# Decode attention on one core: PV moved ahead of the scores, wo split and loaded late, the FFN later

One core of a Trainium2 chip. The metric is the device time of one execution in microseconds. On a single core a run is called slow when it lies over 1.5% above the fastest of the same kernel in the same call; ratios use fast runs only. PE is TensorE, DVE VectorE, ACT ScalarE. The granted clock is the share of PE's full clock that the profile gives for a stretch. A transfer is said to have landed when the last of its 16 completions stands in the trace.

## The reference, cut

Two tokens (batch 2, one position each), 32 heads, a cache of 4096 keys and values per head, head width 128, bfloat16:

```python
q = (x @ wq)                                   # 2 x 512 -> 2 x 32 heads x 128
scores = einsum("bhqd,bhkd->bhqk", q, k_cache) * 128 ** -0.5
p = softmax(scores);  o = einsum("bhqk,bhkd->bhqd", p, v_cache)
a = o.reshape(2, 1, 4096) @ wo                 # 4096 -> 512
b = relu(x @ w1) @ w2                          # 512 -> 1376 -> 512
return g * a + (1 - g) * b                     # g = sigmoid(sum(x * gate_w))
```

K and V are 64 slabs each of 1 MiB (one per batch and head). With wq and wo (4 MiB each), w1 and w2, some 145 MB have to come from HBM.

## The kernel before

A key slab lands as 32 blocks of 128 x 128. PE transposes each block into PSUM (four banks, eight blocks a bank), DVE and ACT copy the banks to `kt`, PE multiplies each transposed block with q (one column), and the softmax of four heads is done together. PV uses the V slab as it landed. Work is laid out in units, one head per unit: in unit k PE does the scores of head k-1, PV of head k-7, and the transposes of head k.

```python
for k in range(NUNITS):                        # PE
    if 1 <= k <= NH:
        unit_scores(k - 1, 0)                  # waits for the copies of head k-1
        unit_scores(k - 1, 1)
    for step, off in (("a", 1), ("b", 2), ("c", 3), ("d", 4)):
        ...                                    # one small softmax matmul in a unit
    unit_pv(k - G - DLY)                       # head k-7: 32 one-column matmuls
    if k < NH:
        unit_trans(k, 0); unit_trans(k, 1)     # 32 transposes
    if k == U_FFN: ffn_setup()                 # U_FFN = 3
pe.wait_ge(S["oT_done"], 1)
for h in range(Hq):                            # all of wo after the last PV
    last = pe.matmul(ATB[0:Bn, 0:D], lhsT=oT_sb[:, h : ... : Hq], rhs=wo_sb[:, h, :], ...)
```

The queue of SyncE issues the loads. A K slab waits for a free buffer out of six, which PE frees; the V slab of head k-6 follows the K slab of head k:

```python
for k in range(NH):
    if k >= NE and (k - NE) - NKR >= 0:
        sp.wait_ge(S["kfree"], k - NKR + 1)    # PE has begun the transposes of head k-5
    sp.dma_start(kdst, kslab(k)).then_inc(ks, 16)
    if k == min(U_FFN - 2, NH - 1): ...        # w1, w2 behind K1
    kv = k - OFFV
    if kv >= 0: issue_v(kv)
```

wo is loaded by ACT's queue as the first thing of the program.

## Time and profile before

| | before |
|---|---|
| time, median of the 4 runs at first | 399.88 us (394.69 to 405.19) |
| time, median of the 16 runs in the end | 405.44 us (394.69 to 411.09) |
| span of the profiled run (the fastest one) | 393.0 us |
| PE busy / granted clock | 85% / 0.716 |
| HBM read | 145.4 MB, 370 GB/s over the span |

From 40 to 340 us PE is busy 90 to 93% of the time and the DMA all of it, so the busy shares decide nothing.

Each run lists its granted clock, and over those of the kernel before the time goes with the clock: 394.69 us at 0.716, 399.12 at 0.708, 403.18 at 0.680.

### The profile page before, as it was taken

To read this page: it belongs to the slowest core of one execution; us is meant where nothing else is said; L and a number is where in the kernel's file an instruction comes from. 1 tells how busy PE (TensorE), PEld (TensorE's weight loads), DVE (VectorE), ACT (ScalarE), POOL (GpSimd) and SP (SyncE) were. 2 spreads that over 40 slices of the span, in tenths; PEclk is the share of its full clock that TensorE was granted. 3 is DMA by queue.
4 is the path that set the end of the run, shared out by engine and by line. 5 is a ranking of instruction groups with operands and counts; after the bars stand their busy time and mean duration, and the time that the engine had idled before them with its cause. 6 is when DMAs were issued, how large, how long until landed. Compare 5 with 4: busy or idle time off the path is not lost.

```text
span 393.0 us, 13993 instructions
## 1 busy us (share of the span) xinstructions
PE 334.4 (85%) x6459; PEld 316.2 (80%) x6459; DVE 163.5 (42%) x326; ACT 73.9 (19%) x184; POOL 1.1 (0%) x8
## 2 busy tenths in 40 slices
PE   0191699899999899999899999999999999998996
PEld 0191678899898899899898989898989898898862
DVE  0030337254434545354545444454545354543511
ACT  1031123221213111221213131312121221213110
POOL 1000000000000000000000000000000000000000
PEclk9997599566857756656868686868685656865658
DMA  8999999999999999999999999999999999999000
GB/s 299 409 386 363 422 420 417 417 419 418 418 419 422 415 419 412 387 389 381 389 404 411 415 409 409 417 403 407 410 415 408 402 386 372 369 419 396 18 3 0
DMA packets 25079, 146.33 MB, mean 372 GB/s; under 512 B 2135, under 2 KB 7613, under 8 KB 8125
## 3 DMA queue, kind: packets, MB, share of 16 engines
q1 hardware_dynamic: 20908, 141.24, 88.9%
q10 hardware_dynamic: 4112, 4.19, 3.3%
q8 instruction: 51, 0.84, 0.8%
q14 instruction: 8, 0.06, 0.0%
HBM read 145.43 MB, written 0.00 MB: 370 GB/s over the span
## 4 chain that ended last, share of the span: by engine, by line
PE 71%; ACT 12%; SPq 7%; DVE 4%; DMA 3%; issue 2%; ACTq 0%; DVEq 0%
PE trb L301 44%; PE otb L372 15%; ACT kt L441 12%; PE scb L329 6%; SPq L221 5%; DMA vnat<-in_A_k_cache_dram 3%; DVE kt L495 3%; PE smb L405 2%; PE smb L356 2%; SPq L220 1%; PE smb L345 1%; PE smb L276 1%; PE smb L352 1%; PE smb L348 0%; PE otb L264 0%
## 5 line engine op out<-in xcount | busy, mean ns | idle before, releaser
L495 DVE COPY kt<-trb 128x1024 bf16<-128x1024 bf16 x207 | 139.6, 690 | 157.2 <-PE trb L301 156.2
L301 PE MATMUL trb<-ident,knat 128*128 128x128 bf16 x1920 | 176.7, 276 | 0.1
L301 PEld LDWEIGHTS trb<-ident,knat 128*128 128x128 bf16 x1920 | 164.3, 128 | 0.4 <-issue 0.3
L441 ACT ACTIVATE kt<-trb 128x1024 bf16<-128x1024 bf16 x49 | 50.2, 1024 | 267.3 <-PE trb L301 267.3
L329 PE MATMUL scb<-qb,kt 128*128 128x1 bf16 x2048 | 75.9, 166 | 26.0 <-ACT kt L441 19.1
L329 PEld LDWEIGHTS scb<-qb,kt 128*128 128x128 bf16 x2048 | 69.0, 102 | 32.9 <-ACT kt L441 24.4
L372 PE MATMUL otb<-pg,vnat 128*128 128x1 bf16 x768 | 23.6, 165 | 0.0
L372 PE MATMUL otb<-pg,vx_wq 128*128 128x1 bf16 x768 | 23.4, 164 | 0.0
L301 PE MATMUL trb<-ident,vnat 128*128 128x128 bf16 x128 | 14.3, 313 | 10.1 <-DMA vnat<-in_A_k_cache_dram 10.1
L372 PEld LDWEIGHTS otb<-pg,vnat 128*128 128x128 bf16 x768 | 21.6, 100 | 0.9
L372 PEld LDWEIGHTS otb<-pg,vx_wq 128*128 128x128 bf16 x768 | 21.4, 99 | 0.7
L301 PEld LDWEIGHTS trb<-ident,vnat 128*128 128x128 bf16 x128 | 13.3, 148 | 10.2 <-issue 10.2
L452 ACT ACTIVATE pg<-scb,negmax 128x32 bf16<-128x32 f32 x64 | 18.3, 331 | 14.0 <-DVE negmax L521 13.9
L249 PE MATMUL otb<-xT_sb,vx_wq 128*128 128x2 bf16 x128 | 3.5, 165 | 15.9 <-DMA vx_wq<-in_A_wq_dram 15.9
L249 PEld LDWEIGHTS otb<-xT_sb,vx_wq 128*128 128x128 bf16 x128 | 3.5, 104 | 15.9 <-issue 15.9
L372 PE MATMUL otb<-pg,vx_w 128*128 128x1 bf16 x512 | 15.7, 165 | 0.0
L372 PEld LDWEIGHTS otb<-pg,vx_w 128*128 128x128 bf16 x512 | 14.4, 100 | 0.6
L535 DVE COPY recipB<-smb 128x4 f32<-128x4 f32 x16 | 2.6, 162 | 29.0 <-PE smb L356 29.0
L452 ACT ACTIVATION_READ_ACCUMULATOR pg<-scb,negmax 128x1 f32 x64 | 12.9, 202 | 0.0
L405 PE MATMUL smb<-wo_sb,oT_sb 128*2 128x512 bf16 x32 | 9.3, 460 | 0.3 <-DVE oT_sb L563 0.3
L521 DVE TENSOR_SCALAR negmax<-smb 128x4 f32<-128x4 f32 x16 | 2.6, 162 | 13.3 <-PE smb L348 13.3
L405 PEld LDWEIGHTS smb<-wo_sb,oT_sb 128*2 128x2 bf16 x32 | 3.1, 98 | 6.1 <-issue 3.2
(41 smaller groups left out, 61.8 us busy)
## 6 DMA issues: line engine op xcount, KB each, us to landing
knat<-in_A_k_cache_dram SPq DMA_DIRECT2D x60, 1024.0 KB, 8.1
vnat<-in_A_v_cache_dram SPq DMA_DIRECT2D x24, 1024.0 KB, 10.2
vx_wq<-in_A_v_cache_dram SPq DMA_DIRECT2D x24, 1024.0 KB, 11.5
vx_w<-in_A_v_cache_dram SPq DMA_DIRECT2D x16, 1024.0 KB, 10.9
wo_sb<-in_A_wo_dram ACTq DMA_DIRECT2D x1, 4096.0 KB, 41.7
vx_wq<-in_A_wq_dram SPq DMA_DIRECT2D x1, 4096.0 KB, 16.7
vnat<-in_A_k_cache_dram SPq DMA_DIRECT2D x4, 1024.0 KB, 17.2
vx_w<-in_B_w_dram SPq DMA_DIRECT2D x1, 1376.0 KB, 27.6
```

What stands on the lines that cost most here:

```text
L220: sp.dma_start(w2_sb[:, 0 : FC - 1, :], w2_main).then_inc(S["ld_w2"], 16)
L221: sp.dma_start(w2_sb[0:FW_LAST, FC - 1, :], w2_tail).then_inc(S["ld_w2"], 16)
L249: last = pe.matmul(PSQ[:, h * Bn : (h + 1) * Bn], lhsT=wq_sb[:, c, h * Dh : (h + 1) * Dh], rhs=xT_sb[:, c * Bn : (c + 1) * Bn], start=(c = ...
L276: last = pe.matmul(PSF[0:Bn, 0:D], lhsT=h1T_sb[0:fw, fc * Bn : (fc + 1) * Bn], rhs=w2_sb[0:fw, fc, :], start=(fc == 0), stop=(fc == FC - 1),)
L301: ins = pe.transpose(TRB[r][:, (jj % 8) * P : (jj % 8 + 1) * P], kb_ap[:, jj * Dh : (jj + 1) * Dh], ident[:, :],)
L329: ins = pe.matmul(bank[:, hg * NBLK + jj : hg * NBLK + jj + 1], lhsT=kt[kk % NKT][:, jj, :], rhs=qb[:, kk : kk + 1], start=True, stop=True,)
L356: pe.matmul(SMB[:, COL_RB : COL_RB + G], lhsT=ones_f[0:G, :], rhs=rdiag[g % 2][:, :], start=True, stop=True).then_inc(S["rbc"], 1)
L372: last = pe.matmul(OTB[:, kp : kp + 1], lhsT=vnat[kp % NVR][:, jj * Dh : (jj + 1) * Dh], rhs=pg[gp % 2][:, jj, hg : hg + 1], start=(jj == ...
L405: last = pe.matmul(ATB[0:Bn, 0:D], lhsT=cols, rhs=wo_sb[:, h, :], start=(h == 0), stop=(h == Hq - 1),)
L441: act.activation(out=kt[k % NKT][:, i * 8 : (i + 1) * 8, :].rearrange("p a b -> p (a b)"), in_=TRB[r][:, :], func=ACT.Copy,).then_inc(trdo ...
L452: act.activation(out=pg[g % 2][:, :, hg], in_=SCB[g % 2][:, hg * NBLK : (hg + 1) * NBLK], func=ACT.Exp, bias=negmax[:, g * G + hg : g * G ...
L495: dve.tensor_copy(out=kt[k % NKT][:, i * 8 : (i + 1) * 8, :].rearrange("p a b -> p (a b)"), in_=TRB[r][:, :],).then_inc(trdone[r], 1)
```

## The change

Its intent: take away PE's waits for the copies, take work out of the tail, and get the K slabs ahead of the weights at the start. From the ninth unit on, PV and the softmax step come before the scores. The wo product is cut in two: heads 0 to 27 of both batches after PV(59), four heads at the end; its accumulator moves to a PSUM bank of the transposes, which are done by then. The wo load is issued by ACT in its unit 46. The FFN runs after unit 6, with w1 behind K4 and w2 behind K5. The rest is bookkeeping (chunks of eight blocks in place of halves, the FFN's output in another bank, an added semaphore). Cut to the core:

```diff
-    U_FFN = 3
+    U_FFN = 6
...
-                if k == min(U_FFN - 2, NH - 1):
+                if k == min(4, NH - 1):
                     sp.dma_start(w1_sb[:], w1_v).then_inc(S["ld_w1"], 16)
+                if k == min(5, NH - 1):
                     sp.dma_start(w2_sb[:, 0 : FC - 1, :], w2_main).then_inc(S["ld_w2"], 16)
...
             for k in range(NUNITS):
-                if 1 <= k <= NH:
-                    unit_scores(k - 1, 0)
-                    unit_scores(k - 1, 1)
-                for step, off in (...): ... softmax_pe(step, kk // G)
-                unit_pv(k - G - DLY)
+                first = k <= G + DLY
+                if first:
+                    ... scores_chunk(k - 1, qi); softmax_pe(step, kk // G)
+                for qi in range(NQ):
+                    pv_chunk(k - G - DLY, qi)
+                if not first:
+                    ... softmax_pe(step, kk // G); scores_chunk(k - 1, qi)
+                if HA > 0 and k - G - DLY == NH - G - 1:
+                    pe.wait_ge(S["oTA"], 1)
+                    pe.wait_ge(S["ld_wo"], 16)
+                    pe.wait_ge(trdone[0], NFILL_SLOT0)
+                    wo_stage(0, HA)
...
-            act.dma_start(wo_sb[:], wo_v).then_inc(S["ld_wo"], 16)      # first instruction of ACT
+                if k == min(46, NH - 1):
+                    act.dma_start(wo_sb[:], wo_v).then_inc(S["ld_wo"], 16)
...
+                if HA > 0 and k == NH + DLY - 1:                         # DVE
+                    dve.wait_ge(S["pvh"], NH - G)
+                    dve.wait_ge(S["rcp"], NG - 1)
+                    dve.tensor_tensor(out=oT_sb[:, 0 : NH - G], in0=OTB[:, 0 : NH - G],
+                                      in1=recipB[:, 0 : NH - G], op=ALU.mult).then_inc(S["oTA"], 1)
```

## The prediction

> **What bounds the kernel now.** I read the page's 40 slices first, then the waits, the windows, the timeline of two heads, and the tail.

> The slices show two engines that are both nearly full:

> ```profile
> PE   0191699899999899999899999999999999998996
> PEclk9997599566857756656868686868685656865658
> DMA  8999999999999999999999999999999999999000
> GB/s 299 409 386 363 422 420 417 417 419 418 418 419 422 415 419 412 387 389 381 389 404 411 415 409 409 417 403 407 410 415 408 402 386 372 369 419 396 18 3 0
> ```

> One slice is 9.8 us. The transfers run up to slice 37 and stop at about 364 us, so the last 29 us (to 393.0) move nothing: a pure tail. In between GB/s is about 419 for a while, then 370 to 410. The busy share of the DMA stays at 1.0 through both, so it cannot tell which side limits. The windows can:

> ```profile
> core 0: us, PE busy (x) PEld busy (x) DVE busy (x) ACT busy (x) POOL busy (x), PEclk, DMA share, GB/s
> 40.00:150.00 110.00, 99.36 (x1888) 94.40 (x1889) 49.65 (x98) 23.84 (x59) 0.00 (x0) 0.70 1.01 419
> 150.00:190.00 40.00, 37.16 (x695) 36.21 (x693) 18.23 (x36) 6.31 (x13) 0.00 (x0) 0.62 1.00 392
> 190.00:300.00 110.00, 101.74 (x2093) 98.23 (x2090) 54.54 (x110) 23.51 (x64) 0.00 (x0) 0.75 1.01 408
> 300.00:340.00 40.00, 36.95 (x721) 35.90 (x720) 17.62 (x36) 8.12 (x20) 0.00 (x0) 0.66 1.00 388
> ```

> GB/s follows the granted clock of TensorE (0.62 and 0.66 give 392 and 388; 0.75 gives 408). One head needs one K and one V slab, 2.10 MB. At 419 GB/s that is 5.0 us; at 388 it is 5.4 us. So from 150 us on PE sets the pace (it frees the K buffers), and from 40 to 150 us the DMA, with a backlog, runs at what I take for its full rate, 419 GB/s. The waits agree: the queue that issues K slabs waits for PE, not the other way round.

> ```profile
> SPq L217 <- PE trb L301: 236.7, 54, 5.6
> ```

> What PE does in a head at half clock (timeline, one unit):

> ```profile
> 356.03 3.57 PE L301 MATMUL trb<-ident,knat 128*128 128x128 bf16 x32
> 359.39 0.82 PE L329 MATMUL scb<-qb,kt 128*128 128x1 bf16 x24
> 360.72 0.38 PE L329 MATMUL scb<-qb,kt 128*128 128x1 bf16 x8 [0.50 <-ACT kt L441]
> 361.14 1.01 PE L372 MATMUL otb<-pg,vnat 128*128 128x1 bf16 x32
> 362.01 3.17 PE L301 MATMUL trb<-ident,knat 128*128 128x128 bf16 x32
> ```

> The unit lasts 362.01 - 356.03 = 5.98 us. The scores follow their own transposes at once, so the last eight wait for the last copy of the transposed keys (ACT, 1.02 us). Over the run:

> ```profile
> PE scb L329 <- ACT kt L441: 19.1, 38, 0.5
> PE scb L329 <- DVE kt L495: 5.7, 27, 0.2
> ```

> Together 24.8 us, 0.39 us a head.

> [...] every stretch of one clock is a multiple of 3.41 us. [...] Windows cut at these boundaries, transposes alone:

> ```profile
> 193.94:197.36 3.42, 1.74 (x18) 1.47 (x15) 0.50 0.97 333
> 197.36:200.77 3.41, 2.96 (x28) 2.96 (x29) 0.50 1.00 408
> 200.77:204.18 3.41, 0.88 (x15) 0.73 (x14) 1.00 1.02 425
> 204.18:207.60 3.42, 2.67 (x27) 2.41 (x24) 0.50 1.02 407
> 207.60:211.01 3.41, 1.79 (x32) 1.79 (x32) 1.00 1.00 413
> ```

> 28 transposes in a window: the next is full speed. 15: the next is half. 27: full. Over all windows the border is near 22 transposes in 3.41 us[...]. [...]

> **The change, part by part.** From the eighth unit on the order is PV(k-7), softmax steps, scores(k-1), transposes(k). All matmuls stay; only where they stand moves.

> (a) Wait of the scores. The copies of head k-1 now have PV (0.86 us to the next stream) and the softmax step in front of the scores. The third DVE copy ends in time, and the ACT copy (1.02 us after about 0.2) ends before the scores come to its eight blocks (0.86 + 24 x 0.027 = 1.5 us). Removed: nearly all of the 24.8 us. The unit at half clock becomes 3.41 (32 x 107 ns) + 0.86 + 0.86 + 0.24 (mean of the softmax steps) = 5.37 us; at full clock 1.82 + 0.86 + 0.86 + 0.2 = 3.7 us.

> (b) Clock. Before, the non-transpose part of a unit at full clock was 2.7 us or more, so a window could hold as few as 13 transposes and the clock fell. Now it is 1.9 us, so any window at full clock and without starving holds at least (3.41 - 1.9)/1.82 x 32 = 26. At half clock the gap of 1.96 us moves through the windows, and at least one window in three holds over 22. So PE runs at 3.7 us per head whenever K is there, less than the 5.0 us of the DMA: the bound passes to the DMA, and PE then waits for K landings.

> (c) DMA floor. Bytes are unchanged, 146.33 MB: 349.2 us at 419 GB/s. Add what cannot be had back: the first 10 us at 298 GB/s lose 2.9 us, and the loads with short rows (slices 3 and 4 at 383 and 368 GB/s, w1, w2, wo) lose 2.1 us. Last V slab landed: 355 us, against 364. So of 25 us of waits removed only 9 us come out of the steady part.

> (d) Start. wq arrives alone, at about 13 us instead of 18; w1 and w2 no longer stand before K2, so the stall of 10.1 us goes:

> ```profile
> PE trb L301 <- DMA vnat<-in_A_k_cache_dram: 10.1, 1, 10.1
> ```

> PE reaches its first PV at 50 to 55 us rather than 65.7. That is no gain of its own in a DMA-bound run, but it lets PE arrive at the end with no backlog. wo at unit 46 costs 10 us of DMA there, already inside the 349.2.

> (e) Tail. Before, PE is some six heads behind when the transfers stop, and then come

> ```profile
> 380.63 9.27 PE smb L405 x32
> ```

> 32 wo matmuls. After, 28 of them stand behind PV(59). V59 lands four slabs, 10 us, before the end: 345. PV, multiply: 346.4. The 28 matmuls: before, they came every 0.43 us at half clock for 4.5 us, then 0.215; so 8.3 us, to 354.7. PV(60) to PV(63): 4 x 0.96, to 358.5, and 0.5 for the last softmax steps: 359. Multiply 0.5, four wo matmuls 1.3 and drain 0.4, two DVE operations 1.5, output transfer 1.6 (all from the old tail): 364.3 us. I add 2 us for a PE that lags by part of a unit: span 366. The profiled run took 1.7 us more than its span (394.69 to 393.0): 368 us.

> **Rivals.** *The clock stays half.* If the shorter unit locks to the windows at half clock, PE stays the bound: first PV at 55, 57 heads x 5.37 us = 361, then seven PV units without transposes (7), the wo block (8.3) and the end (6): 382, so 384 us measured, 4% faster. For it: the old kernel does lock, to 20.5 us (six windows) for four heads. Against: the count in (b) leaves no such phase. *The DMA does not hold 419.* It dropped to 408 and below wherever PE was slow, but I read that as lack of demand; if part of it is the DMA's own (say 408 throughout), the floor grows by 9.4 us: 377 us. *The wo load starves PE.* If K is late by 10 us at unit 46 and PE cannot make it up, the end moves by up to 10 us: 378. Against: 17 units follow in which PE has 1.3 us a unit in hand, and the bytes were in the old run too. *Copies take over.* DVE needs 3 x 0.85 = 2.55 us a head and ACT 1.02, below 3.7; this one I discard.

> **Range and chances.** The centre is the DMA floor plus the new tail, 368. Below 361 there is no room: it would need more than 419 GB/s. The upper end, 381, holds the slower-DMA and wo rivals and part of the clock rival. Since the old runs spread from 394.7 to 405.2 around 399.88, faster by over 2% means below 391.9, which even the worst rival reaches: 0.95. Within 2%: 0.04. Slower: 0.01.

> **What would show it.** Right: GB/s 415 to 420 from slice 5 to the end; PE waiting for K landings on the transposes' line; waits of the scores for the copies below 5 us; less than 12 us between the last landing and the end; four heads per 20 us. Wrong: scores still waiting; GB/s at 400 with PE never waiting for K; clock at half nearly throughout with units of 5.4 us; or an idle PE near unit 46 that is never made up.

## The result

| | before | after |
|---|---|---|
| time, median | 405.44 us (16 runs, 394.69 to 411.09) | 372.96 us (11 runs, 371.59 to 373.68) |
| span of the profiled run | 393.0 us | 371.0 us |
| granted clock | 0.716 | 0.758 |
| last V slab landed | 365.6 us | 362.8 us |
| from there to the end | 27.4 us | 8.2 us |

The ratio of the fast runs is 0.937 (95% interval 0.933 to 0.941). A ratio is the mean time of one kernel's fast runs over that of the other's of the same rounds, so not quite the ratio of the medians, which is 0.920 here: the fast runs of the kernel before are those below 400.6 us, a quarter of its 16. Both profiles are of fast runs, and the one of before is of its very fastest, so the two traces show a smaller gap (22 us) than the medians (32 us).

The spread is a result of its own. The changed kernel's runs have clocks from 0.742 to 0.780 and all lie within 2.1 us; its time no longer goes with PE's clock.

The slices of the page of the changed kernel (9.3 us each):

```profile
PEclk9999888886689588885888866888856585665667
...
GB/s 275 427 408 382 411 420 416 416 419 417 420 417 420 415 416 420 417 418 421 419 415 420 415 419 420 416 418 404 409 408 409 406 408 406 406 412 421 394 191 5
```

And its windows (busy time of each engine, then granted clock, DMA share, GB/s):

```profile
50.00:150.00 100.00, 94.50 (x2003) 92.23 (x2004) 51.01 (x103) 21.30 (x55) 0.00 (x0) 0.76 1.01 418
150.00:190.00 40.00, 36.95 (x768) 35.92 (x766) 19.30 (x39) 8.52 (x22) 0.00 (x0) 0.74 1.01 418
190.00:250.00 60.00, 54.89 (x1135) 53.04 (x1131) 29.45 (x58) 12.78 (x33) 0.00 (x0) 0.77 1.01 418
...
300.00:340.00 40.00, 35.54 (x675) 34.35 (x673) 16.68 (x34) 8.52 (x22) 0.00 (x0) 0.63 1.02 410
```

The stretch from 150 to 190 us, where the kernel before fell to 392 GB/s at a clock of 0.62, now holds 418. From 250 to 340 us it is 408 to 410: there the wo load runs beside K and V.

The waits of the changed kernel (line, releaser: us in total, times, longest):

```profile
PE trb L308 <- DMA knat<-in_A_k_cache_dram: 17.4, 23, 2.1
...
PE scb L334 <- DVE kt L526: 1.2, 5, 0.2
...
PE scb L334 <- ACT kt L470: 0.5, 1, 0.5
```

The 24.8 us of score waits are 1.7 us, and PE now waits for K slabs (23 times), which it did not do even once on the K ring before. One stretch of its timeline (start, length, engine, line):

```profile
204.80 3.01 PE L308 MATMUL trb<-ident,knat 128*128 128x128 bf16 x28
...
207.60 1.03 PE L361 MATMUL otb<-pg,vx_w 128*128 128x1 bf16 x32
...
208.69 0.95 PE L334 MATMUL scb<-qb,kt 128*128 128x1 bf16 x32
...
209.54 1.95 PE L308 MATMUL trb<-ident,knat 128*128 128x128 bf16 x32
...
214.53 2.75 PE L308 MATMUL trb<-ident,knat 128*128 128x128 bf16 x30 [0.43 <-DMA knat<-in_A_k_cache_dram]
```

The scores run in one piece right behind PV, and two transposes in a row start 214.53 - 209.54 = 4.99 us apart, which is the time of 2.10 MB at 420 GB/s: PE walks at the pace of the DMA. This is what the prediction asked to see.

The end of the changed kernel: 28 wo matmuls, the last PV, the last four wo matmuls.

```profile
352.83 9.03 PE L396 MATMUL trb<-wo_sb,oT_sb 128*2 128x512 bf16 x28 [0.39 <-DVE oT_sb L581]
...
364.83 0.96 PE L361 MATMUL otb<-pg,vx_w 128*128 128x1 bf16 x32
...
366.04 1.87 PE L396 MATMUL trb<-wo_sb,oT_sb 128*2 128x512 bf16 x4 [0.25 <-DVE oT_sb L600]
```

One thing was not foreseen. The last slab lands at 362.8 us, 8 us after the 355 us of the prediction. The trace has the 16 completions of each transfer one by one. I take each for one DMA engine's part: with eight of the last slab's still to come the DMA share was 0.49 to 0.59 (352 to 360 us), and with one of them left, in the run with more fetches below, 0.06. For a slab that lands at 45.8 us they lie within 2.0 us; for one at 184.4 us within 6.6; for the last one within 11.3: eight of them come between 351.5 and 355.5 us, the other eight between 360.8 and 362.8. The windows show the same: the DMA share falls to a half at 352 us and stays there for eight.

```profile
352.00:353.00 1.00, 0.61 (x15) 0.42 (x12) 0.30 (x2) 0.33 (x3) 0.00 (x0) 0.50 0.55 229
...
358.00:359.00 1.00, 1.00 (x5) 0.33 (x4) 0.00 (x0) 0.00 (x0) 0.00 (x0) 0.71 0.52 205
...
360.00:361.00 1.00, 1.00 (x6) 0.40 (x5) 0.00 (x0) 0.00 (x0) 0.00 (x0) 1.00 0.26 107
```

### The profile page after: what moved, and what is told of

Read it like the earlier page. It is cut to its first block, busy times and chain, and to the rows that moved or that the text cites.

```text
span 371.0 us, 13995 instructions
## 1 busy us (share of the span) xinstructions
PE 322.2 (87%) x6459; PEld 303.2 (82%) x6459; DVE 162.4 (44%) x327; ACT 73.9 (20%) x184; POOL 1.1 (0%) x8
## 2 busy tenths in 40 slices
DMA packets 25078, 146.33 MB, mean 394 GB/s; under 512 B 2134, under 2 KB 7612, under 8 KB 8124
## 4 chain that ended last, share of the span: by engine, by line
DMA 54%; PE 33%; SPq 9%; issue 2%; DVE 2%; ACT 0%; DVEq 0%
DMA knat<-in_A_k_cache_dram 37%; PE trb L308 16%; DMA vx_w<-in_A_v_cache_dram 9%; DMA vx_wq<-in_A_v_cache_dram 8%; PE otb L361 6%; PE scb L334 5%; SPq L228 4%; PE trb L396 3%; SPq L223 3%; DVE kt L526 1%; SPq L217 1%; PE otb L283 1%; SPq L227 1%; PE smb L386 0%; PE otb L271 0%
## 5 line engine op out<-in xcount | busy, mean ns | idle before, releaser
L308 PE MATMUL trb<-ident,knat 128*128 128x128 bf16 x1920 | 173.3, 272 | 19.3 <-DMA knat<-in_A_k_cache_dram 17.4
L308 PEld LDWEIGHTS trb<-ident,knat 128*128 128x128 bf16 x1920 | 160.9, 126 | 21.3 <-issue 20.8
L334 PE MATMUL scb<-qb,kt 128*128 128x1 bf16 x2048 | 64.1, 164 | 3.0 <-DVE kt L526 1.2
L334 PEld LDWEIGHTS scb<-qb,kt 128*128 128x128 bf16 x2048 | 57.7, 98 | 6.5 <-ACT kt L470 1.7
L361 PEld LDWEIGHTS otb<-pg,vnat 128*128 128x128 bf16 x768 | 23.5, 102 | 4.3 <-issue 2.2
L256 PE MATMUL otb<-xT_sb,vx_wq 128*128 128x2 bf16 x128 | 3.6, 165 | 11.7 <-DMA vx_wq<-in_A_wq_dram 11.7
L256 PEld LDWEIGHTS otb<-xT_sb,vx_wq 128*128 128x128 bf16 x128 | 3.5, 104 | 11.7 <-issue 11.7
L396 PE MATMUL trb<-wo_sb,oT_sb 128*2 128x512 bf16 x32 | 10.9, 515 | 0.6 <-DVE oT_sb L581 0.4
L558 DVE RECIPROCAL rcp_sb<-smb 4x1 f32<-4x1 f32 x16 | 2.5, 156 | 18.7 <-PE smb L382 18.5
L308 PE MATMUL trb<-ident,vnat 128*128 128x128 bf16 x128 | 9.3, 241 | 0.0
L396 PEld LDWEIGHTS trb<-wo_sb,oT_sb 128*2 128x2 bf16 x32 | 3.2, 105 | 7.1 <-issue 4.7
L308 PEld LDWEIGHTS trb<-ident,vnat 128*128 128x128 bf16 x128 | 8.7, 110 | 0.0
## 6 DMA issues: line engine op xcount, KB each, us to landing
vx_wq<-in_A_wq_dram SPq DMA_DIRECT2D x1, 4096.0 KB, 12.5
```

Of the source, the lines that this page charges most:

```text
L256: last = pe.matmul(PSQ[:, h * Bn : (h + 1) * Bn], lhsT=wq_sb[:, c, h * Dh : (h + 1) * Dh], rhs=xT_sb[:, c * Bn : (c + 1) * Bn], start=(c = ...
L308: ins = pe.transpose(TRB[r][:, (jj % 8) * P : (jj % 8 + 1) * P], kb_ap[:, jj * Dh : (jj + 1) * Dh], ident[:, :],)
L334: ins = pe.matmul(bank[:, hg * NBLK + jj : hg * NBLK + jj + 1], lhsT=kt[kk % NKT][:, jj, :], rhs=qb[:, kk : kk + 1], start=True, stop=True,)
L361: last = pe.matmul(OTB[:, kp : kp + 1], lhsT=vnat[kp % NVR][:, jj * Dh : (jj + 1) * Dh], rhs=pg[gp % 2][:, jj, hg : hg + 1], start=(jj == ...
L396: last = pe.matmul(ATB[0:Bn, 0:D], lhsT=cols, rhs=wo_sb[:, h, :], start=(h == 0), stop=(h == Hq - 1),)
```

## Experiments

The theory: the order of a unit gave PE room, so the DMA became the bound; the wo split shortened the tail; the moved loads are worth nothing by themselves. Rivals: the start is what mattered; the split is what mattered; PE still sets the pace. A second question came with the late last landing: instruction fetches. The page lists 51 packets of 16 KB for instructions; each took about 1.07 us in the trace, they came mostly one every 6 to 8 us, and their durations repeat with a period of eight (from the second eight to the sixth, the seventh and eighth of each took 1.02 to 1.03 us, the other six 1.06 to 1.11). That eight engines take them in turn was my guess from this; the trace does not name the engines.

| run | median us (runs) | against 372.96 |
|---|---|---|
| kernel before + new order alone | 376.94 (4) | +4.0 |
| changed kernel, old order | 389.95 (4) | +17.0 |
| changed kernel, wo not split | 377.73 (4) | +4.8 |
| changed kernel, wo loaded at the start | 372.50 (4) | -0.5 |
| changed kernel, FFN and w1, w2 early | 372.71 (4) | -0.3 |
| changed kernel, 4 PV matmuls in place of 32 | 365.90 (4) | -7.1 |
| changed kernel, more instructions to fetch | 379.54 (4) | +6.6 |
| changed kernel, half V slabs | 339.88 (4) | -33.1 |
| the same with the old order | 395.24 (4) | +22.3 |
| two V slabs in pieces of 8 rows, in the middle | 390.00 (4) | +17.0 |
| the same, the last two slabs | 381.44 (4) | +8.5 |

The 372.96 is from other calls than these runs, which were made on four chips, so differences under about 1 us say nothing; within each kernel of this table that is bound by the DMA the runs agree within 0.5%. Each call ran the kernel before as well (medians 406.7, 406.5, 408.1 and 405.5). The ratios of one kernel move with which of its runs of before count as fast (0.937 to 0.917 for the same 372 to 373 us), so I compare levels.

### The order alone

```diff
 # kernel before
+                first = k <= G + DLY
+                if not first:
+                    unit_pv(k - G - DLY)
-                if 1 <= k <= NH:
+                if first and 1 <= k <= NH:
                     unit_scores(k - 1, 0); unit_scores(k - 1, 1)
                 ... softmax step ...
-                unit_pv(k - G - DLY)
+                if not first and 1 <= k <= NH:
+                    unit_scores(k - 1, 0); unit_scores(k - 1, 1)
+                if first:
+                    unit_pv(k - G - DLY)
```

> The kernel before with one edit: from the ninth unit on PE runs PV, softmax step, scores, transposes. Theory (the order frees PE, the DMA becomes the bound): waits of the scores for copies fall from 24.8 us to under 5, GB/s stays near 418 until the transfers end, the last slab lands at 360 to 364 us; no wo split, so PV(63) at 365 and then 0.5 + 9.3 + 0.3 + 1.5 + 1.6 us: span 378, time 378 to 382 (ratio to the kernel before some 0.95). Rival (the start is what matters: wo and w1/w2 out of the way of the first heads): 395 or more, no change. Rival (the gain is the wo split in the tail): no change either.

Measured: 376.94 us (ratio to the kernel before 0.938, 0.931 to 0.945), span 375.1. The last slab landed at 361.8 us, GB/s stayed at 415 to 423 from slice 6 to the end of the transfers, and the groups show the waits of the scores gone (busy us, mean ns, idle us before and what ended it):

```profile
L329 PE MATMUL scb<-qb,kt 128*128 128x1 bf16 x2048 | 64.0, 164 | 5.0 <-issue 2.2 <-DVE kt L502 1.2 <-ACT kt L448 1.0
```

PV(63) started at 361.81, right after its slab, and the 32 wo matmuls took 8.94 us from 363.14. That is a little below the expected 378 to 382 us, because PV(63) started at 361.8 and not at 365. Some ten lines in one loop are 28.5 of the 32.5 us between the medians of the kernel before and the changed one; by the fast runs alone they are 25.0 us (mean 402.2 to 377.2). Both rivals fall as accounts of the main gain.

### The changed kernel with the old order

```diff
-                first = k <= G + DLY
+                first = True
```

> The changed kernel with the old order kept in all units (scores, softmax step, PV, transposes); loads, FFN place and wo split as changed. Theory: PE is the bound again, the scores wait 20 us or more, GB/s falls below 410 in some stretches, and the time is 385 to 398 with the wide spread of the kernel before; only the wo split (about 6 us) and the start are gained. Rival (start or split are what matters): 376 or less.

Measured: 389.95 us, three runs from 388.89 to 390.71 at clocks of 0.684 to 0.688 and a slow one of 397.18 at 0.657: the spread of a PE-bound kernel is back. In its profile GB/s falls to between 357 and 396 in slices 20 to 28, and the scores wait:

```profile
L334 PE MATMUL scb<-qb,kt 128*128 128x1 bf16 x2048 | 75.7, 166 | 27.1 <-ACT kt L470 22.0 <-DVE kt L526 4.5
```

The 16 completions of its last slab lie within 5.3 us, not 11.3.

This run also shows that the parts do not add up. Without the new order, the wo split and the moved loads together still gain 12.6 us (fast runs: 402.2 to 389.6), twice the 6 us that the expectation gave to the split; the first PV starts at 49.3 us in place of 65.7. Where PE is the bound an early start can count; how the 12.6 us divide between start and split was not tested.

### wo in one piece

```diff
-    HA = Hq - G if (NH - G) // Hq == Bn - 1 else 0
+    HA = 0
```

> The changed kernel with all 32 wo matmuls after the last PV. Last landing unchanged, about 363 us; PV(60) to PV(62) are done before it, PV(63) ends at about 364; then multiply 0.5, 32 wo matmuls 9.3, two DVE operations 1.8, output 1.6: span 377, time 379, 6 us more than the changed kernel. If the split is worth nothing because PE still has other work there: 373. If it is worth all of the gain: 395 or more.

Measured: 377.73 us, span 376.5, last landing 362.3. The split is worth 4.8 us, 1 us less than expected: in the changed kernel the 28 matmuls hold PE until 361.9 us, so that PV(60) to PV(63) end at 365.8, 2 us later than the slabs alone would allow.

### The loads of the start

wo at the start:

```diff
+            act.dma_start(wo_sb[:], wo_v).then_inc(S["ld_wo"], 16)
             act.wait_ge(S["q_ps"], 1)
...
-                if k == min(46, NH - 1):
-                    act.dma_start(wo_sb[:], wo_v).then_inc(S["ld_wo"], 16)
```

> The changed kernel with the wo load issued at the start, as before the change. Theory (DMA-bound from the start to the end, bytes unchanged): the wo bytes move from the stretch 245 to 335 us to the first 45 us; K0 lands later by some 4 us and PE starts later, but makes it up; end within 3 us of the changed kernel (370 to 376). GB/s near 418 from 50 us to the end. Rival (moving wo out of the start is a main gain): 380 or more.

FFN after unit 3, its weights behind K1:

```diff
-    U_FFN = 6
+    U_FFN = 3
-                if k == min(4, NH - 1):
+                if k == min(1, NH - 1):
-                if k == min(5, NH - 1):
+                if k == min(1, NH - 1):
```

> The changed kernel with the FFN after unit 3 and w1, w2 loaded behind K1, as before. Theory: PE waits some 5 to 8 us for K2 again, but the DMA keeps the end: within 1.5 us of the changed kernel. Rival (the start matters): 5 us or more slower.

Measured: 372.50 and 372.71 us, last landings 361.4 and 362.4. Neither move is worth anything, though both do what they were meant to do locally (q's wait for wq is 11.7 us with wo late, 16.0 with wo first; with the early FFN PE waits 3.1 us for K2, less than the 5 to 8 expected). In this kernel, bound by the DMA from start to end, these two shifts of bytes do not matter: PE made up even a first PV at 63.3 us (wo first) in place of 50.7.

### Is PE still the bound? Less PV work

```diff
-                for jj in range(qi * nper, (qi + 1) * nper):
+                for jj in range(qi * nper, qi * nper + 1):
```

> The changed kernel with 4 instead of 32 PV matmuls a head (wrong result on purpose). PE loses 28 x 27 ns = 0.75 us a head, 48 us in all, and 3584 of its 12918 instructions. If PE still sets the pace: 330 to 345. If the DMA does (theory): the bytes are the same, the last landing stays within 357 to 363 and the time within 365 to 373; of this, a few us may come from fewer instruction fetches [...]: 51 fetches become about 37, so the slow engines end some 2 us sooner and the spread of a slab's 16 completions at the end falls from 11 to about 8 us.

Measured: 365.90 us. The record marks the result as correct although seven eighths of the PV products are left out, so its check does not notice that; why is not shown. PE lost some 48 us of work and the time fell by 7.1: PE is not the bound. GB/s is the same 415 to 422 before the wo load and 406 to 409 beside it. The last landing moved from 362.8 to 359.4, and the spread of its 16 completions from 11.3 to 7.9 us, as expected for the fetches. The page of the changed kernel and of this run, instruction packets (count, MB, share):

```profile
q8 instruction: 51, 0.84, 0.9%
```

```profile
q8 instruction: 37, 0.61, 0.7%
```

The rest comes after the last landing (4.7 us to the end in place of 8.2), where four PV units are shorter. The experiment shortens PE and takes fetches at once, so it does not prove the fetches by itself; the next one adds instructions to fetch and nothing else.

### More fetches and nothing else

```diff
             ).then_inc(S["c_ident"], 1)
+            for _ in range(6000):
+                pool.wait_ge(c1, 1)
```

> The changed kernel with 6000 satisfied waits on the idle GpSimd queue: nothing but instructions to fetch, 384 KB, about 23 fetches of 16 KB more on some of the DMA engines. Theory (fetches make some engines fall behind, and the slowest engine sets the last landing): the last landing moves by about 23/8 x 1.1 us = 3 us if they fall on the same 8 engines, or not at all, with a smaller spread of the 16 completions, if they fall on the other 8. If fetches have nothing to do with the spread: spread 11 us and time as in the changed kernel.

Measured: 379.54 us, runs from 378.81 to 379.80: 6.6 us slower through instructions that do nothing on an idle engine. The 24 packets that came with them (8 KB each, 192 KB in place of the expected 384) show under another queue, which had seven before:

```profile
q14 instruction: 31, 0.25, 0.2%
```

In the trace one completion of each slab falls back steadily, all others stay as they were: of the last slab's 16, fifteen are there within 11.0 us of the first and the sixteenth at 17.1, at 368.7 us. The windows show what is left then, a DMA share of 0.06 (1 in 16) and 25 GB/s:

```profile
362.00:363.00 1.00, 1.00 (x4) 0.31 (x3) 0.00 (x0) 0.00 (x0) 0.00 (x0) 0.50 0.06 25
364.00:365.00 1.00, 1.00 (x4) 0.34 (x3) 0.00 (x0) 0.00 (x0) 0.00 (x0) 0.50 0.06 25
```

I had allowed for 3 us or none; all of the delay fell on one completion, so it was more. So with 24 more instruction packets and the same transfers one completion came 6.1 us after the other fifteen, and the last landing moved with it from 362.8 to 368.7 us. That PE's 51 fetches hold back eight engines in the same way is my inference from the eight late completions (360.8 to 362.8 us); it is not shown. The wo load is not the cause: with wo at the start the last spread is 11.0 us all the same.

The packets' own time does not cover the lag. The 50 fetches before the end of the transfers, 1.07 us each, would be 6.7 us for each of eight engines, but the two halves end 9.0 us apart (means 352.4 and 361.4 us). The 24 extra packets took about 0.34 us each, 8.1 us in all; the last slab now has seven early completions, eight late ones and the one at 368.7, so by these counts the late one came from the early half (mean 352.4) and fell back by some 16 us, an estimate. If the fetches are the cause, they cost more than their packets show, and why stays open.

### What PE can do when K is there

From V16 on only half of each V slab is loaded (meant to give a wrong result), once with the new order of a unit and once with the old one:

```diff
-                sp.dma_start(vnat[kv % NVR], vslab(kv)).then_inc(vsem[kv % NVR], 16)
+                if kv < NVR:
+                    sp.dma_start(vnat[kv % NVR], vslab(kv)).then_inc(vsem[kv % NVR], 16)
+                else:
+                    sp.dma_start(vnat[kv % NVR][:, 0 : SLAB // 2], vslab(kv)[:, 0 : SLAB // 2]).then_inc(...)
```

(The bound in the code is NVR = 11, so the halves begin at V11, not at V16 as the expectation says.)

> The changed kernel with only half of each V slab loaded from V16 on (wrong result on purpose): 25 MB less, 1.57 MB a head, 3.75 us of DMA at 418 GB/s. It shows what PE can do when K is there. If PE locks to the full clock as I predicted (3.7 us a head): PE and DMA tie, granted clock above 0.9, time 305 to 320. If PE alternates between the clocks at some 4.5 us a head: 335 to 350, PE never waiting for K. If PE were the bound already at 5 us: 365 or more.

> The run with half V slabs (339.9 us with the new order) once more, with the old order of a unit (wrong result on purpose). The DMA needs 3.75 us a head here, so PE alone sets the pace in both, and the pair gives the pace of PE itself with each order. In the half-V run with the new order heads came every 4.6 us. If the order is what gave PE its room: 5.1 to 5.6 us a head with the old one, the scores waiting 20 us or more for copies, granted clock below 0.75, time 370 to 395. If PE has the same pace with both orders (then the gain of the change came from elsewhere): 338 to 345.

Measured: 339.88 us with the new order, 395.24 with the old one (385.04 to 398.02; the one fast run is 385.04, the profiled one, 398.02, counts as slow beside it). The transposes between 150 and 290 us, new order first, then old (busy and count of PE, of its weight loads, then clock, DMA share, GB/s):

```profile
150.00:290.00 140.00, 81.41 (x973) 75.45 (x971) 0.76 0.98 373
```

```profile
150.00:290.00 140.00, 80.09 (x798) 74.75 (x795) 0.62 0.80 289
```

32 transposes are a head: 140 x 32 / 973 = 4.60 us a head against 140 x 32 / 798 = 5.61. The second is from the slow profiled run; the fast one, 385.0, has no trace, but is still 45 us above the new order. PE waited for the K ring once, for 1.6 us, in each, and with the old order the scores waited 26.5 us for copies. Of the 1.01 us between the two paces the waits for copies are 0.39 (26.5 and 1.7 us over 64 heads); the rest comes with the granted clock, 0.62 against 0.76. So the order lifts PE's own pace from above the 5.0 us that the DMA needs to below it. It does not lift it to 3.7: in the trace with the new order PE holds the full clock for one to five windows of 3.41 us, then a window with only 22 or 23 transposes comes (195.0 to 198.4 us, for instance; six of the eight such ends between 150 and 290 us), and the next one to four run at half. The full-speed windows that kept the clock had 24 or more.

### An attempt to even out the engines

Two V slabs were sent as sixteen transfers of eight rows, slabs 25 and 45 in one run, 62 and 63 in the other, meant to give work to eight of the 16 engines only, 2.5 us a slab more for these and as much less for the others (my assumption; the runs do not show it):

```diff
+    V8 = (25, 45)                              # or (62, 63)
+                else:
+                    for p0 in range(0, P, 8):
+                        sp.dma_start(vnat[kv % NVR][p0 : p0 + 8, :], vslab(kv)[p0 : p0 + 8, :]).then_inc(...)
```

> The changed kernel with two V slabs (25 and 45) sent as sixteen transfers of 8 partitions each in place of one of 128. [...] Theory (the last landing is late because half of the engines lost 9 to 11 us to instruction fetches): if the 8 that take the rows are the fast half, the spread of the last slab's 16 completions falls from 11 to 2 us, the last landing from 363 to 358 and the time to 368 to 370; if they are the slow half, the spread grows to 20 us and the time to 377 to 379; if the two halves cut across each other, little changes. If the spread does not matter for the end: 372 to 374 with a changed spread.

> The same for the last two V slabs, 62 and 63. The last landing should move as in the run with slabs 25 and 45 (358 or 368), but K63 and V58 to V61 land as late as before, so PE, which has the wo block and four PV units to do after V59, would end at 365 anyway: if the slabs go to the fast half, the time stays at 371 to 373; if to the slow half, 377.

Measured: 390.00 and 381.44 us. Both lie outside every outcome that was expected, and both failed as experiments. The small transfers slowed everything: in the first run GB/s fell to 236 to 238 from 165 to 175 us, and the pieces of V25, eight completions each, came in over 15 us (163.5 to 178.6). The 16 completions of the next K slab lay 14.0 us apart, those of later ones 9.5, and at the end 19.3, in other groups than before (two, eleven and three). A slab in sixteen pieces cost several times its 2.5 us (17.0 us more for two slabs in the first run); why, and which engines eight rows go to, these runs do not tell. No version that beats the changed kernel came out.

## Why the prediction was right, and where not

The measured 372.96 us lie within 361 to 381, 5 us above the 368, and the forecast of 8.0% (368.0 to 399.88) is what the medians show (372.96 to 405.44, 8.0%). That the two agree to the decimal is luck: the kernel before came out 5.6 us slower over 16 runs than in the 4 at first, and the changed kernel missed by 5.0. Against the 399.88 the change is 6.7%, and by the fast runs 6.3%.

*(a) The waits of the scores.* Right: 24.8 us became 1.7. (The "eighth unit" of the prediction is unit 8, the ninth.)

*(c) The DMA floor.* The rate held: 418 GB/s from 50 to 250 us, where the kernel before fell with PE's clock. The last landing came at 362.8 and not 355, and this term is the whole of the error. Two parts: beside the wo load the rate is 408 for 90 us, which costs 90 x (1 - 408/418) = 2.2 us, more or less what the prediction had counted for short rows; and the 16 completions of the last slab do not come together. Their mean is 356.9, 2 us from the predicted 355, and the last one is 6 us later. The step that failed is the unspoken one that bytes over rate gives the last landing: here it came within 2 us of the mean of the completions, and the last of them moved when the instruction packets did (37 in place of PE's 51: 359.4; 24 more on another queue: 368.7).

*(d) The start.* As predicted in its local effects (wq landed at 14.0 us for 13, the wait for K2 went, the first PV came at 50.7 us), and as predicted worth nothing: undoing either half of it changed the time by less than 0.5 us. Beside the wo load wq came at three quarters of the rate that it has without (16.7 us to landing with it, 12.5 without).

*(e) The tail.* From last landing to end 9.3 us were predicted and 8.2 measured. The 28 wo matmuls took 9.03 us for 8.3, but since the landings were late they ran beside the last four slabs. The prediction's chain ran from V59 on, and there it fits better still: V59 landed at 351.3 for 345, and from it to the end 19.7 us were measured and 19.3 predicted, before the 2 us added for a lagging PE, which were hardly needed.

*The rivals.* "The clock stays half" did not come about with PE at 4.60 us a head. "The DMA does not hold 419" is refuted up to 250 us, and so is my doubt whether the dips of the kernel before were lack of demand: they were. "The wo load starves PE" is half true: 10.0 of PE's 17.4 us of K waits are between 245 and 340 us, with heads 5.8 us apart, and it still costs nothing (wo at the start: 372.50).

So where did the gain come from? Put first, the order gives 28.5 us by the medians (25.0 by fast runs) and the rest 4.0, of which the split accounts for all (4.8 without it) and the loads for nothing. Put last, on top of split and loads, the order gives 17.0 (16.6 by fast runs). It is the largest part either way. In the traces of the fastest run of before and of the changed kernel the last landing hardly moved (365.6 to 362.8), and the gain sits in the tail (27.4 to 8.2 us): PE had run six heads behind the transfers and no longer does. That is 19.2 us out of 22; the prediction had 9 us coming out of the steady part. In the usual runs of the kernel before, with clocks of 0.65 to 0.69, PE was slower still.

## What to carry over

When two resources are both nearly full, move work until one of them waits for the other, and read which rate goes with which clock; here a reordering that removed 0.39 us of wait per head, and raised the granted clock (0.62 to 0.76 with half V slabs), moved PE across the DMA's pace of 5.0 us a head (5.61 to 4.60) and made the time steady as well as shorter. Once this kernel was bound by its transfers, moving two loads changed the time by less than 0.5 us, and two things were left: the tail behind the last landing (8.2 us), and the latest of the 16 completions. Half of them came 9 us late, and with 24 more instruction packets one came 17.1 us after the first. And a gain split among parts of a change depends on which part comes first.
